# Counts of zero products on TensorE in a two-stage attention and wave-MLP kernel

## The chip, the cores and the metric

The kernel runs on one core of one Trainium2 chip. The metric is the device time of one execution in microseconds (us). The engines are named as in the profile: PE is TensorE's matrix products and PEld its weight loads, DVE is VectorE, ACT is ScalarE, POOL is GpSimd, SP is the engine that issues most transfers. L344 is line 344 of the kernel.

## The reference

Two blocks follow each other. The first is an attention with polynomial features, over 4 batches, 4 heads, 1088 positions and a head size of 32; the second mixes 1088 positions with two matrices, over the 128 channels that the heads make together.

```python
def phi(x):
    a = np.einsum('rd,bhsd->bhsr', S1, x)      # r = 8
    b = np.einsum('rd,bhsd->bhsr', S2, x)
    return np.einsum('bhsi,bhsj->bhsij', a, b).reshape(*x.shape[:-1], r * r)
q_p, k_p = (phi(q), phi(k))
kv = np.einsum('bhsf,bhsd->bhfd', k_p, v)
z = np.sum(k_p, axis=2)
num = np.einsum('bhsf,bhfd->bhsd', q_p, kv)
den = np.einsum('bhsf,bhf->bhs', q_p, z)[..., None] + 1e-06
x = num / den                                  # heads joined: (4, 1088, 128)
theta = x @ w_theta
y = einsum('ts,bsd->btd', w_tok_r, x * cos(theta)) + einsum('ts,bsd->btd', w_tok_i, x * sin(theta))
u = x + y
out = u + np.maximum(u @ w_ch, 0.0)
```

The arrays arrive in the types of the host; the matrices of the second block are 8-byte floats, which the kernel turns into 4-byte floats itself.

## The kernel before

Every step is recorded first as an operation with its engine, its buffers and a function that emits the instructions, and has a number. A list written out by hand, `SEQUENCE`, gives the order in which the recorded operations are emitted, and with it the order on each engine; each engine works through its own in order. A second list, `PLACES`, gives each buffer its slot, so a tile that is written again waits for the readers of the tile before in that slot. A third, `FILLS`, says in front of which operations PE gets extra products whose operands are zeroes and whose result nobody reads. A positive count writes the tile `nowhere`; a negative count writes the PSUM slot that the operation is about to use, which is asked for anew for each of these products:

```python
for o in self.order:
    n = self.fills.get(o.i, 0)
    for _ in range(n):
        fill()
    for b in o.bufs:
        if b.ap is None:
            b.ap = view(pools[b.cls](b.slot), b.shape, b.dt)
            if n < 0 and b.cls == "ps":
                for _ in range(-n):
                    fill(pools[b.cls](b.slot)[:, :GW_FILL])
                n = 0
    o.fn()
```

One such product (a fill, L378) is 128 x 128 weights by 384 columns in a 2-byte type. Eleven of them are an operation of their own at the very start, as soon as POOL has set `idle` to zero (L380). `FILLS` adds eight in front of operation 12.

The first operations, in PE's order of before: the 19 fills; operation 12, the transpose L431 of a small maximum `m` of the sketch matrices, for which DVE (L432, then L328) works out a power of two; the transposes L770 of the first batch of keys; four fills; the product L344 with `ones` that spreads that power of two; the transposes L993 of queries and L770 of keys; two fills; further transposes; a product for the size of the queries; and then the products of the first batch's rounded keys with themselves (`hf`, then `big`). Meanwhile ACT squares the keys with their sum (L673) and the queries (L969); DVE (L328) takes the step of the rounding from the keys' sum, rounds the keys and subtracts what was rounded (L324).

The middle, where the first stage ends: for each batch DVE multiplies the features of the queries out in three parts (tiles `g`, from `lv`, L324), PE transposes each part in two groups of three (L1127), ACT copies these (L1131), and PE multiplies them with the batch's keys and values. Operation 741 is the first such group of three of one batch; nine fills stand in front of it. The third part of a batch goes into the slot of its first part. Between these steps stand the unpacking of the matrices of the second block (ACT L609 and L611 from the loaded `zs` tiles, DVE L328 and L324, some additions as transfers by POOL, L338) and the products of the second block, `ps<-big,zs`, L344.

From about 107 us on, these products of the second block follow each other to the end, with a sum of matrix quarters in place of some of the products, and the output is stored batch by batch.

Of the kernel before, what the change touches and what calls it, by code (L numbers as in the profile page):

```python
# [116 lines left out]
)  # L117
FILLS = (
    (12, 8), (15, 4), (65, 1), (741, -9),
)  # L120


# [1434 lines left out]
```

## Time and profile before

| | us |
|---|---|
| median of 3 runs | 226.09 |
| lowest and highest | 226.06, 226.94 |
| profiled execution | 226.22 |
| its span, from the first to the last instruction | 224.4 |

| engine | busy us | share of the span | instructions |
|---|---|---|---|
| PE | 218.4 | 97% | 1502 |
| PEld | 181.6 | 81% | 1502 |
| DVE | 173.9 | 77% | 414 |
| ACT | 124.2 | 55% | 259 |
| POOL | 62.1 | 28% | 98 |

A share of busy time is a mean over stages with different limits, and a product of zeroes counts as busy. The 34 fills show as L378 with the tile `idle`; their profile groups have 9.9 us of busy time together. In a line of the timeline, the first figure is the start, the second the time to the end of the last of the merged instructions, and the bracket holds the idle time of that engine just before it, with the instruction that ended it.

### The profile page before, as it was taken

What the parts mean: (1) busy time and instruction counts of PE and PEld (TensorE: products, weight loads), DVE (VectorE), ACT (ScalarE), POOL (GpSimd) and SP (SyncE); (2) the same over time, 40 slices, a digit from 0 to 9 for tenths busy, and PEclk for the clock granted to TensorE, in tenths of its full rate; (3) what the DMA queues carried; (4) which work ended last, traced back from release to release, by engine and by line L of the source; (5) the groups of instructions that cost most, each with busy time, mean ns of one, the idle gap of its engine ahead of it and who ended that gap; (6) DMA issues with size and microseconds to landing.
All of it is one profiled execution on the core that took longest, in us unless ns stands there. A gap on an engine that the chain in (4) does not pass through costs nothing.

```text
span 224.4 us, 4128 instructions
## 1 busy us (share of the span) xinstructions
PE 218.4 (97%) x1502; PEld 181.6 (81%) x1502; DVE 173.9 (77%) x414; ACT 124.2 (55%) x259; POOL 62.1 (28%) x98
## 2 busy tenths in 40 slices
PE   7999999999999999999999999999999999999993
PEld 3798999998897496778888887888888888888882
DVE  3699999999999799999989987479770626723653
ACT  3898899599999599899989904760000000000000
POOL 1198920000007033048460277429500000000000
PEclk9999999999999999999999999999999999999999
DMA  3999999999459996998999799979992002341223
GB/s 116 413 418 407 410 339 329 409 417 423 130 191 256 267 286 186 195 251 159 192 239 324 135 182 196 193 128 183 190 181 48 0 0 37 66 71 28 50 41 61
DMA packets 31800, 45.71 MB, mean 204 GB/s; under 512 B 18852, under 2 KB 19108, under 8 KB 31652
## 3 DMA queue, kind: packets, MB, share of 16 engines
q1 hardware_dynamic: 24580, 30.30, 38.4%
q0 software_dynamic: 7200, 15.14, 37.2%
q8 instruction: 12, 0.20, 0.4%
q14 instruction: 8, 0.07, 0.1%
HBM read 28.07 MB, written 2.23 MB: 135 GB/s over the span
## 4 chain that ended last, share of the span: by engine, by line
PE 94%; DVE 3%; issue 1%; POOL 0%; DVEq 0%; POOLq 0%
PE ps L344 82%; PE ps L378 4%; PE ps L1127 2%; PE ps L1075 2%; PE ps L770 2%; PE ps L993 2%; DVE big L324 1%; DVE big L328 1%; DVE zs L324 0%; DVE sm L331 0%; DVE sm L328 0%; PE ps L938 0%; POOL idle L380 0%; DVE g L324 0%; PE ps L951 0%
## 5 line engine op out<-in xcount | busy, mean ns | idle before, releaser
L344 PE MATMUL ps<-big,zs 128*128 128x288 f32 (+2 forms) x498 | 115.6, 386 | 0.1
L344 PEld LDWEIGHTS ps<-big,zs 128*128 128x128 f32 x498 | 90.9, 190 | 20.3 <-DVE big L328 0.6
L338 POOL DMA_DIRECT2D big<-big x41 | 38.0, 1411 | 87.4 <-ACT sm L785 39.0
L609 ACT ACTIVATE big<-zs 128x544 f32<-128x544 f32 x32 | 22.1, 710 | 0.4 <-DVE big L324 0.3
L611 ACT ACTIVATE big<-zs 128x1088 int32<-128x1088 uint32 x16 | 19.2, 1217 | 0.0
L331 DVE SCALAR_TENSOR_TENSOR big<-ps,even,big 128x288 f32<-128x288 f32 (+2 forms) x23 | 10.6, 480 | 6.0 <-PE ps L344 5.8
L328 DVE TENSOR_SCALAR big<-big 128x544 int32<-128x544 int32 (+1 forms) x33 | 14.6, 461 | 0.5 <-ACT big L609 0.5
L344 PE MATMUL ps<-mf,big 128*128 128x96 f32 x72 | 14.4, 295 | 0.0
L331 DVE SCALAR_TENSOR_TENSOR big<-ps,big 128x288 f32<-128x288 f32 (+1 forms) x15 | 6.4, 439 | 10.1 <-PE ps L344 10.1
L338 POOL DMA_DIRECT2D big<-hf x9 | 12.9, 1928 | 0.1
L324 DVE TENSOR_TENSOR zs<-ps,g 128x768 f32<-128x768 f32 (+2 forms) x20 | 12.6, 629 | 0.1
L324 DVE TENSOR_TENSOR g<-lv 128x768 f32<-128x768 f32 x12 | 11.1, 954 | 1.8 <-PE ps L1127 1.7
L344 PEld LDWEIGHTS <-hf 128*128 128x128 f16 (+1 forms) x144 | 11.9, 106 | 0.5 <-issue 0.2
L324 DVE TENSOR_TENSOR big<-big,ps 128x288 f32<-128x288 f32 (+1 forms) x12 | 5.1, 427 | 8.6 <-PE ps L344 8.6
L378 PE MATMUL ps<-idle 128*128 128x384 bf16 x34 | 9.9, 415 | 1.8 <-POOL idle L380 1.3
L344 PE MATMUL ps<-w,big 128*128 128x128 f32 (+1 forms) x76 | 11.4, 285 | 0.0
L324 DVE CUSTOM_DVE_ANT_0 big<-big,big 128x1088 uint16<-128x1088 uint16 x16 | 11.3, 714 | 0.0
L344 PE MATMUL ps<-big,big 128*128 128x128 f32 x72 | 11.0, 283 | 0.0
L344 PEld LDWEIGHTS ps<-mf,big 128*128 128x128 f32 x72 | 10.9, 191 | 0.2 <-issue 0.2
L324 DVE TENSOR_TENSOR big<-big,hf 128x1152 f32<-128x1152 f32 x8 | 10.9, 1368 | 0.1
L344 PEld LDWEIGHTS ps<-w,big 128*128 128x128 f32 x76 | 9.8, 191 | 1.2 <-issue 0.6
L344 PE MATMUL ps<-mv,hf 128*128 128x96 f16 x108 | 10.6, 206 | 0.0
(196 smaller groups left out, 387.6 us busy)
## 6 DMA issues: line engine op xcount, KB each, us to landing
zs<-w_tok SPq DMA_DIRECT2D x17, 1088.0 KB, 12.2
big<-big POOLq DMA_DIRECT2D x40, 272.0 KB, 6.8
big<-k_l SPq DMA_DIRECT2D x7, 576.0 KB, 8.0
big<-q_l SPq DMA_DIRECT2D x4, 576.0 KB, 9.9
big<-v_l SPq DMA_DIRECT2D x4, 576.0 KB, 9.2
big<-hf POOLq DMA_DIRECT2D x3, 576.0 KB, 11.6
big<-hf POOLq DMA_DIRECT2D x6, 272.0 KB, 12.2
out<-g SPq DMA_DIRECT2D x32, 36.0 KB, 1.7
```

The lines of the kernel that those rows point to most:

```text
L324: eng.tensor_tensor(out=o, in0=a, in1=b, op=f)
L328: (eng or V).tensor_scalar(out=o, in0=a, scalar1=s1, scalar2=s2, op0=op0, **kw)
L331: (eng or V).scalar_tensor_tensor(out=o, in0=a, scalar=s, in1=b, op0=op0, op1=op1)
L338: op("G", n * 2.55e-3, lambda: G.dma_start(dst(), src(), accum_op=ALU.add), w, r, kind=2)
L344: T.matmul(o, lhs, rhs, start=start, stop=stop, skip_group_check=True)
L378: T.matmul(nowhere() if out is None else out, idle()[:, 0:P], idle(), start=True, stop=True, skip_group_check=True)
L609: op("A", 0.19 + HT * 0.0009, lambda j=j: A.activation(dst[j](), words()[1][:, j * HT:(j + 1) * HT].bitcast(F32), AF.Prelu, scale=scale, a ...
L611: op("A", 0.22 + S * 0.0009, lambda: A.activation(stp().rearrange("p r n -> p (r n)"), words()[0].bitcast(U32), AF.Copy, scale=2.0**-29), ...
L770: T.transpose(tr()[:, i * P:(i + 1) * P], kx()[:, g * GC + i].rearrange("p h d -> p (h d)"), ident())
L993: T.transpose(tr()[:, i * P:(i + 1) * P], x()[:, g * GC + i].rearrange("p h d -> p (h d)"), ident())
L1075: T.transpose(x()[:, i], xs()[:, off + i * P:off + (i + 1) * P], ident())
L1127: T.transpose(tr()[:, i * P:(i + 1) * P], qp()[:, i * H + 2 * n:i * H + 2 * n + 2].rearrange("p h i j -> p (h i j)"), ident())
```

## The change

Only the table of counts changes:

```diff
 FILLS = (
-    (12, 8), (15, 4), (65, 1), (741, -9),
+    (102, 3), (291, 3), (65, 1), (741, -4),
 )
```

The eleven fills at the very start stay. None follow them in front of L431 now; three stand between L431 and the first transposes L770 (operation 102), and three between the product with `ones` and the transposes L993 (operation 291), where four stood before that product. In front of operation 741 there are four instead of nine. The order of all other instructions, their buffers and the transfers are the same: PE has 11 products fewer, and as many weight loads.

## The prediction

> **What bounds the kernel now.** I read the page first: TensorE (PE) is busy 97% of the span. That is no answer yet, since products of zeroes count as busy. So next the busy time by stretches, for which engine has no idle time where:
>
> ```profile
> core 0: us, PE busy (x) PEld busy (x) DVE busy (x) ACT busy (x) POOL busy (x), PEclk, DMA share, GB/s
> 7.80:77.30 69.50, 68.69 (x663) 61.32 (x662) 67.24 (x164) 62.96 (x140) 21.95 (x47) 1.00 0.94 336
> 77.30:79.10 1.80, 1.63 (x11) 1.08 (x11) 0.12 (x2) 0.07 (x1) 0.00 (x0) 1.00 1.02 416
> 79.10:107.00 27.90, 27.78 (x217) 21.90 (x216) 27.46 (x54) 26.61 (x58) 11.17 (x14) 1.00 0.87 211
> 107.00:220.00 113.00, 113.00 (x587) 93.62 (x585) 75.55 (x165) 31.34 (x57) 27.71 (x32) 1.00 0.65 123
> ```
>
> Up to 107 us VectorE (DVE) works nearly without a pause, 67.24 of 69.50 us and 27.46 of 27.90; in the 1.80 us between, it does 0.12. After 107 us PE alone is full. So the time is a DVE stage, then a PE stage: what brings DVE forward in the first brings PE's start of the second forward. The list of waits on DVE confirms that the early stage has few holes. Its largest entries (15.9 and 15.0 us behind PE L344) cannot lie before 107 us, since DVE idles only 2.26 and 0.44 us there; these two can, and are the only waits that fills end:
>
> ```profile
> DVE sm L432 <- PE ps L431: 2.6, 1, 2.6
> DVE g L324 <- PE ps L1127: 1.7, 1, 1.7
> ```
>
> The timeline of the start (start, duration, engine, line, operation, idle time before it):
>
> ```profile
> 1.34 5.64 PE L378 MATMUL ps<-idle 128*128 128x384 bf16 x19 [1.34 <-POOL idle L380]
> ...
> 5.80 0.15 PEld L378 LDWEIGHTS <-idle 128*128 128x128 bf16 x1 [0.17 <-issue]
> 6.12 0.48 PEld L378 LDWEIGHTS <-idle 128*128 128x128 bf16 x3 [0.17 <-issue]
> 6.43 1.17 ACT L673 ACTIVATE big<-big 128x1152 f32<-128x1152 f32 x1 [1.69 <-DMA big<-k_l]
> ...
> 6.82 0.27 PE L431 MATMUL ps<-ident,m 128*2 128x128 f32 x1
> ...
> 7.13 0.28 DVE L432 TENSOR_REDUCE sm<-ps 2x1 f32<-2x128 f32 x1 [2.60 <-PE ps L431]
> ...
> 7.50 0.19 ACT L673 ACTIVATION_READ_ACCUMULATOR big<-big 128x1 f32 x1
> ...
> 8.14 0.32 DVE L328 TENSOR_SCALAR sm<-sm 128x1 int32<-128x1 int32 x2
> ```
>
> Nineteen fills hold PE until 6.82 us; only then comes the small transpose L431, whose operand DVE finished at 4.53 us (4.37 + 0.16, L450). Note the spacing of the weight loads: 0.32 us up to 6.12, then three in 0.48. PE runs at half pace until about 6.2 us, though the clock column prints 1.00.
>
> The timeline of the gap:
>
> ```profile
> 74.70 3.35 PE L378 MATMUL ps<-idle 128*128 128x384 bf16 x9
> ...
> 75.52 1.83 DVE L324 TENSOR_TENSOR g<-lv 128x768 f32<-128x768 f32 x2
> ...
> 78.12 1.53 PE L1127 MATMUL ps<-ident,g 128*128 128x128 f32 x12
> 79.03 1.25 ACT L1131 COPY g<-ps 128x384 f32<-128x384 f32 x3 [2.74 <-PE ps L1127]
> 79.03 0.96 DVE L324 TENSOR_TENSOR g<-lv 128x768 f32<-128x768 f32 x1 [1.68 <-PE ps L1127]
> ```
>
> DVE has its first product of lv ready at 75.52 + 0.96 = 76.48, but the transposes that read it start at 78.12, behind nine fills. DVE's third product goes into the first one's tile, so it waits for the six transposes that read that tile. ScalarE (ACT) waits beside it.
>
> **The change, part by part.** All sums are against the profiled execution: 226.22 us, a span of 224.4 and 1.82 around it. It lies 0.13 above the median of 226.09.
>
> *The gap, 9 fills to 4.* In the chain that ended last the fills stand at 75.09, 75.46, 75.84 and so on, 0.378 apart, because each waits for the one before on the same PSUM tile. Five fewer would free PE 1.9 us earlier: the fourth of them ends at 76.18. But then DVE's product at 76.48 is last. Where PE waits for such a product elsewhere (92.61 + 0.96 = 93.57, transposes at 93.71) 0.14 passes; after a fill, 0.04. So the transposes start at 76.52 to 76.62, the six take 0.89 as before, and DVE's third product starts 0.03 later, at 77.44 to 77.54 instead of 79.03. That is 1.49 to 1.59; I take 1.5. DVE's own second product ends at 77.35 (75.52 + 1.83), so 0.1 to 0.2 of the wait of 1.68 remains. ACT's copy at 79.03 moves by as much.
>
> *Does the 1.5 us last?* Next late is DVE itself, without holes to 107 us, then PE without holes. What could hold them is data that does not move along. The loads of w_tok (L604) issued at 72.81 and 75.84 take 7.4 us at most, so the later lands by 83.2. ACT first reads this pair at 87.14, or 85.3 when moved by 1.8: 2 us of cover; if it were gone, each us over would return as DVE idle time. The additions by DMA are issued by GpSimd when DVE or PE is ready, so they move too. I take all of it.
>
> *The start, 19 and 4 to 11, 3 and 3.* Eleven fills at 0.32 end at 1.34 + 3.52 = 4.86 us. L431 follows at once, 1.96 earlier; three more fills (0.96) end near 6.1, before the keys land (ACT's wait ends at 6.43). DVE's row of small operations, 7.13 to 8.22, goes to about 5.2 to 6.3. The operation at 8.14 needs only ACT's sum, ready at 7.50 + 0.19 = 7.69, so it starts at 7.72: 0.42 us. The two groups of three after it stand in place of four; they end before the square of the queries does (8.89 + 0.19 = 9.08), for which the next small product waits, so I cost them at nothing. If that cover were gone, two fills at half pace would cost 0.64.
>
> Not all of the 0.42 lasts. ACT waits for loads at 6.43 and at 7.82, and from there to 19.13 it idles for some 0.1 us, so it hardly moves. ACT L832 (18.62 + 0.42 = 19.04) gates PE's product at 19.36, which gates DVE at 20.02. PE can come 0.2 to 0.3 earlier there, and DVE has 0.13 of its own to lose. I take 0.3. The bounds are 0 (ACT holds all) and 0.9: how long the 19 fills take depends on when the pace doubles, and the runs shown differ by 0.88 (226.06 to 226.94).
>
> The sum: 1.5 + 0.3 = 1.8, so 226.22 − 1.8 = 224.4.
>
> **The clock, which speaks against the change.** The clock column is 1.00 throughout; half pace shows only in the spacing of 0.32 us before 6.2. In the gap of before PE gets one fill per 0.378 us, and the pace still held: the six transposes behind the fills take 0.89 us. With four fills, PE's stretch from 74.87 to 77.4 holds four fills and six transposes, with idle times of at most 0.4 us between them. By rows, then, no fall, and no term in the sum. The Trainium skill ("TensorE: Matmul & The Clock Gate", Part 1) says that the array starts at half clock, is let up by sustained activity, and falls back after an idle window of some 3.4 us; its Part 4 adds that transposes do not count as busy in the same way. By that rule the transposes that take the place of the five fills might count as idle, and the gap could become the place of a fall, which is the third rival below. No run here shows such a fall; the trace agrees with the slow start alone.
>
> **The rivals.**
> 1. *Transfers do not come forward.* GpSimd's additions wait for one another: the waits have POOL behind DMA for 7.9 us in three waits, and DVE behind DMA once, 0.5 us. If those after 107 us are paced by their queue, up to 1.8 us returns there as that wait, less what PE's queued work hides. Against it: the DMA share is 0.65 after 107 us and 0.87 before. Half lost: 225.3.
> 2. *The pace doubles late at the start.* Fewer fills before 6.2 us could delay the doubling. PE's work from 8.27 to 9.7 would then take 1.4 us more, and the first large product (10.92) would slip by up to that, while the early 0.3 is lost: 226.22 − 1.5 + 0.9 = 225.6, taking part as covered by PE's slack. Against it: fills, keys' transposes and fills follow each other in the changed order with 0.4 us of idle time.
> 3. *Slower: the clock falls in the gap.* Place: from the first transposes at 76.5. At the start half pace lasted from 1.34 to 6.2, 4.9 us; the same length here, in work that is 27.78 of 27.90 us PE, loses 2.4 us: 226.22 − 1.8 + 2.4 = 226.8. It decides against the change once half pace lasts over 3.6 us, and shows as slower once it lasts over 5.6. For a fall that lasts 6 us, between one length and two, it is 227.4, which I take. For it: five fills that kept PE busy go. Against: PE's idle time stays under 0.4 us at a time.
> 4. *The start brings more*, 0.9 instead of 0.3: 223.8.
>
> That the counts do not reach the program is no rival: the built order of PE has 11 fills, L431, 3, L770, L344, 3, and four in the gap.
>
> **How the numbers follow.** The forecast has 0.66, rival 1 0.10, rival 2 0.07, rival 3 0.11, rival 4 0.06. The likeliest is 224.4. Half a per cent of the median, about what a measurement of this kernel can tell from no change, is 1.13 us: faster is below 224.96, slower above 227.22. Faster: 0.64 of the forecast, 0.06 of rival 4, 0.04 of the halves of rivals 1 and 2: 0.74. Slower: most of rival 3, 0.09. The rest, 0.17, is the same. The range goes from 223.7, just past rival 4, to 225.9, past rivals 1 and 2; it leaves out rival 3 and the odd tails, some 0.17.
>
> **What would show it.** Right: L431 near 4.9 us; the wait of DVE L432 at about 0.7 instead of 2.6; DVE L328 at 7.7 instead of 8.14; four fills from about 74.4; L1127 right behind DVE's first product; the wait of DVE g L324 for L1127 at 0.1 to 0.2 instead of 1.7; PE's L344 of 84.98 near 83.2; the stretch to the end as long as before. Wrong: weight loads of fills 0.32 apart past 7 us or L344 products at twice their time after 76 us (rivals 2, 3); a DVE or ACT wait for DMA after 80 us (rival 1); no earlier DVE at 20 us (the early term is 0).

## The result: 224.73 us, and a wider spread than before

The changed kernel has a median of 224.73 us over 22 executions (224.09 to 228.07), the kernel before 226.26 over 22 (225.74 to 227.01): a ratio of 0.994, 95% interval 0.9921 to 0.9959. So it is faster, by 0.6%, and near the 224.4 of the forecast: 1.53 us were gained where 1.8 were forecast. But where these executions of before lie within 1.3 us of each other, those of the changed kernel do not: 14 lie from 224.09 to 225.26 (called short below), six from 225.61 to 226.89 (called long), two at 228.0. The ratio leaves out the two at 228.0, which had a granted clock of 0.99 and left no trace, and nothing below explains them. The profiled execution took 226.89 us (span 225.1), 0.67 more than the one before. It holds both the gain and what ate it.

The start, in the timeline of the changed kernel:

```profile
1.34 3.70 PE L378 MATMUL ps<-idle 128*128 128x384 bf16 x11 [1.34 <-POOL idle L380]
...
4.83 0.42 PE L431 MATMUL ps<-ident,m 128*2 128x128 f32 x1
...
5.29 0.28 DVE L432 TENSOR_REDUCE sm<-ps 2x1 f32<-2x128 f32 x1 [0.66 <-PE ps L431]
...
7.51 0.34 DVE L328 TENSOR_SCALAR sm<-sm 128x1 int32<-128x1 int32 x2 [1.13 <-ACT big L673]
```

The small transpose comes 1.99 us earlier, and the step of the rounding (L328) starts at 7.51 instead of 8.14. What holds it now is ACT's sum, as forecast.

The gap:

```profile
76.96 1.46 PE L378 MATMUL ps<-idle 128*128 128x384 bf16 x4
...
77.78 1.83 DVE L324 TENSOR_TENSOR g<-lv 128x768 f32<-128x768 f32 x2
...
78.88 1.72 PE L1127 MATMUL ps<-ident,g 128*128 128x128 f32 x12 [0.47 <-DVE g L324]
...
79.77 1.41 ACT L1131 COPY g<-ps 128x384 f32<-128x384 f32 x3 [1.22 <-PE ps L1127]
79.77 0.96 DVE L324 TENSOR_TENSOR g<-lv 128x768 f32<-128x768 f32 x1 [0.16 <-PE ps L1127]
```

DVE's first product ends at 77.78 + 0.96 = 78.74, and the transposes follow at 78.88. DVE's third product waits 0.16 us, where it waited 1.68. Ahead of the gap the whole kernel runs late, 77.78 against 75.52 for DVE's first product, +2.26; behind it +0.74, 79.77 against 79.03. The gap gave 1.52. In stages, cut at the corresponding places of the changed kernel:

```profile
7.80:79.60 71.80, 68.09 (x662) 61.19 (x661) 67.10 (x162) 62.71 (x140) 19.59 (x45) 1.00 0.92 325
79.60:79.80 0.20, 0.17 (x3) 0.08 (x2) 0.04 (x2) 0.04 (x1) 0.00 (x0) 1.00 0.94 392
79.80:107.70 27.90, 27.90 (x218) 22.21 (x219) 27.46 (x54) 26.71 (x58) 11.14 (x14) 1.00 0.93 234
107.70:220.70 113.00, 113.00 (x587) 93.62 (x586) 75.48 (x165) 31.26 (x57) 27.70 (x32) 1.00 0.65 123
```

The columns are those of the stretches of before: length, busy time of PE, PEld, DVE, ACT and POOL, then the clock. The last two stretches are as long as before and as full, 27.46 of 27.90 us for DVE and 113.00 of 113.00 for PE. In the first, DVE does 67.10 us of work as before (67.24), in 71.80 us instead of 69.50. There the time went, and PE's timeline shows the place:

```profile
31.80 0.33 PE L344 MATMUL ps<-sm,ones 128*128 128x1 f32 x2
34.80 1.53 PE L344 MATMUL ps<-g,big 128*64 128x128 f32 x24 [2.67 <-ACT big L609]
```

Before, the same product started with no wait:

```profile
32.25 1.53 PE L344 MATMUL ps<-g,big 128*64 128x128 f32 x24
```

The page names ACT L609, one of which ran from 34.10 to 34.80 us. But the product does not need that one: before, it started at 34.34, two us after the product. One operand of the product is the first batch's values, which SP loads with an issue at 14.87 us. The trace's semaphore records have the last part of this load at 34.67, 0.13 us before the product starts; before, it was there at 30.14, 2.1 us ahead of the product. Experiments below name that load outright, again with 0.14 us between its last part and the product. The clock is not it: behind the stall the 24 products take 1.53 us, as in a short execution of the change (from 31.80 us there). GpSimd's order had moved as well. GpSimd before, then after:

```profile
20.50 2.01 POOL L324 TENSOR_TENSOR mv<-c,hm 128x32 f16<-128x32 f16 x4
22.48 1.03 POOL L324 TENSOR_TENSOR mf<-cf,hm 128x32 f32<-128x32 f32 x2
23.45 1.06 POOL L338 DMA_DIRECT2D big<-hf  x1
```

```profile
19.88 0.83 POOL L324 TENSOR_TENSOR mv<-c,hm 128x32 f16<-128x32 f16 x4
20.67 0.44 POOL L324 TENSOR_TENSOR mf<-cf,hm 128x32 f32<-128x32 f32 x2
21.05 1.05 POOL L338 DMA_DIRECT2D big<-hf  x1
```

GpSimd was 0.6 us ahead, but its first addition by DMA (L338, 576 KB) went out 2.4 us ahead, since its small products took 1.2 instead of 3.0 us. The theory to test is this: the gap saves 1.5 us always; the start saves a few tenths, but in some executions lets this addition out early, and it takes DMA time from the load of the values that was queued first. Rival A: that load is late by chance, whatever the addition does. Rival B: the clock falls in some executions.

### The profile page after: what moved, and what is told of

Same layout as the page of the kernel before. It is cut to its first block, busy times and chain, and to the rows that moved or that the text cites. A ratio compares the mean times of both kernels' runs of the same rounds, so it can differ in the third digit from the quotient of the medians.

```text
span 225.1 us, 4106 instructions
## 1 busy us (share of the span) xinstructions
PE 216.3 (96%) x1491; PEld 180.4 (80%) x1491; DVE 174.3 (77%) x414; ACT 124.1 (55%) x259; POOL 60.0 (27%) x98
## 4 chain that ended last, share of the span: by engine, by line
PE 71%; DVE 17%; DMA 5%; ACT 2%; SPq 2%; issue 1%; DVEq 0%
PE ps L344 66%; DVE g L324 5%; DMA big<-q_l 4%; PE ps L1127 3%; DVE sm L331 2%; DVE big L328 2%; DVE sm L324 1%; DVE big L324 1%; PE ps L1075 1%; DVE lv L324 1%; SPq L651 1%; DVE hf L328 1%; PE ps L770 1%; DVE zs L324 1%; DMA out<-g 1%
## 5 line engine op out<-in xcount | busy, mean ns | idle before, releaser
L338 POOL DMA_DIRECT2D big<-big x41 | 38.0, 1410 | 87.0 <-ACT sm L785 40.8
L609 ACT ACTIVATE big<-zs 128x544 f32<-128x544 f32 x32 | 22.3, 715 | 0.9 <-DMA zs<-w_tok 0.6
L328 DVE TENSOR_SCALAR big<-big 128x544 int32<-128x544 int32 (+1 forms) x33 | 14.4, 455 | 0.5 <-ACT big L609 0.5
L338 POOL DMA_DIRECT2D big<-hf x9 | 12.9, 1918 | 3.2 <-DMA big<-k_l 3.1
L324 DVE TENSOR_TENSOR zs<-ps,g 128x768 f32<-128x768 f32 (+2 forms) x20 | 12.5, 626 | 0.1
L344 PE MATMUL ps<-g,big 128*64 128x128 f32 x144 | 9.2, 277 | 2.7 <-ACT big L609 2.7
L324 DVE TENSOR_TENSOR big<-big,ps 128x288 f32<-128x288 f32 (+1 forms) x12 | 5.1, 426 | 8.6 <-PE ps L344 8.6
L324 DVE TENSOR_TENSOR g<-lv 128x768 f32<-128x768 f32 x12 | 11.1, 951 | 0.3 <-PE ps L1127 0.2
L324 DVE CUSTOM_DVE_ANT_0 big<-big,big 128x1088 uint16<-128x1088 uint16 x16 | 11.2, 712 | 0.0
L324 DVE TENSOR_TENSOR big<-big,hf 128x1152 f32<-128x1152 f32 x8 | 11.0, 1370 | 0.1
```

What stands on the lines that cost most here:

```text
L324: eng.tensor_tensor(out=o, in0=a, in1=b, op=f)
L328: (eng or V).tensor_scalar(out=o, in0=a, scalar1=s1, scalar2=s2, op0=op0, **kw)
L338: op("G", n * 2.55e-3, lambda: G.dma_start(dst(), src(), accum_op=ALU.add), w, r, kind=2)
L344: T.matmul(o, lhs, rhs, start=start, stop=stop, skip_group_check=True)
L609: op("A", 0.19 + HT * 0.0009, lambda j=j: A.activation(dst[j](), words()[1][:, j * HT:(j + 1) * HT].bitcast(F32), AF.Prelu, scale=scale, a ...
```

## The experiments

The kernels ran in three groups of four, each group on one chip with its own runs of before: medians of before are 226.28 (the two halves, addition later, addition earlier), 226.49 (the four from "change again" on) and 226.42 (the last four). In these groups the executions of before spread over 1.4 to 1.7 us. All times are medians, with the range, in us; ratios are against before.

| kernel | time | ratio, 95% interval |
|---|---|---|
| gap alone | 224.90 (224.27 to 225.52) | 0.9933 (0.9909 to 0.9957) |
| start alone | 225.91 (225.46 to 229.52) | 0.9983 (0.9966 to 1.0) |
| change, addition later | 224.22 (224.01 to 225.12) | 0.9909 (0.9884 to 0.9933) |
| before, addition earlier | 227.71 (227.03 to 230.91) | 1.0075 (1.0043 to 1.0108) |
| change again | 224.49 (224.10 to 224.77) | 0.9903 (0.9880 to 0.9925) |
| later, no fills in the gap | 224.50 (224.19 to 225.65) | 0.9915 (0.9889 to 0.9940) |
| later, no fills at the start | 225.56 (225.03 to 225.78) | 0.9952 (0.9932 to 0.9973) |
| change, values before queries | 224.68 (224.25 to 224.97) | 0.9911 (0.9890 to 0.9932) |
| change, addition forced early | 225.75 (225.41 to 227.79) | 0.9977 (0.9955 to 1.0) |
| forced early, values first | 225.38 (225.12 to 225.70) | 0.9945 (0.9926 to 0.9965) |
| change, third time | 224.38 (224.17 to 226.27) | 0.9913 (0.9881 to 0.9944) |
| change, addition later, again | 224.53 (224.01 to 224.68) | 0.9901 (0.9878 to 0.9925) |

**The two halves, each alone.**

```diff
 gap alone
-    (12, 8), (15, 4), (65, 1), (741, -9),
+    (12, 8), (15, 4), (65, 1), (741, -4),
 start alone
-    (12, 8), (15, 4), (65, 1), (741, -9),
+    (102, 3), (291, 3), (65, 1), (741, -9),
```

> The counts of the start stay as before (8 in front of operation 12, 4 in front of 15); only the nine in the gap become four. Theory (the gap gives 1.5 us in every execution; the lower values of the change come from it; the long executions of the change come from the start, whose earlier additions by DMA hold back the load of the first batch's values): about 224.7 us, 1.5 less than the kernel before, and its executions lie as close together as those of before (within 1.3 us); PE near 32 to 35 us has no stall before ps<-g,big. Rival A (the load of the values is late by chance, whatever the start): as widely spread as the change, 224.2 to 226.9. Rival B (long executions come from a clock that falls in the gap): widely spread too, with L344 or L1127 products at twice their time after 76 us in a long one.

> The counts of the start are those of the change (3 in front of operations 102 and 291); nine stay in the gap. Theory: median 0.1 to 0.3 us below the kernel before, and widely spread, with executions up to 2.5 us above the shortest; where a profile falls on a long one, PE waits 2 to 3 us before ps<-g,big near 32 us. Rival A: as widely spread as before plus what chance gives every kernel of this call alike. Rival B: as close together as before, since nine fills keep the gap busy.

The gap alone gains 1.38 us in the median, the start alone 0.37, with an interval that reaches no change; together 1.75, where the forecast had 1.5 and 0.3. The seven executions of the gap alone lie within 1.25 us of each other, as the theory had it. In the trace of the gap alone, DVE starts 0.39 us earlier than before in front of the gap and 1.91 earlier after it: 1.52 for the gap. Its 0.39 at the start is no work of the change, since its counts there were those of before: its 19 fills took 4.60 us instead of 5.64, since PE's pace doubled earlier. The start alone is less spread than expected: 11 of 12 executions lie within 225.46 to 226.79, one at 229.52. So the long executions came less often here than in the change, and this run alone does not show that they come from the start.

In the trace of the start alone the load of the values shows itself in the chain that ended last (start, duration):

```profile
14.96 17.02 DMA big<-v_l
```

It ends at 31.98, and PE's product behind it starts at 32.12, 0.38 us later against before than the instructions ahead of it. So the load can be the last to arrive even with the addition at 22.94 us. In the two short profiles of the change, below, its last part lands 0.9 us before PE's product: that is all the cover it has there.

**The addition moved, later and earlier.** GpSimd's order of operations: 23 are the products mv<-s, mv<-c and mf<-cf, 241 the first addition, 26 and 20 the small copies behind it, 139 the second addition.

```diff
 counts of the change, addition later
-   30, 23, 241, 26, 20, 139
+   30, 23, 26, 20, 241, 139
 counts of before, addition earlier
-   19, 30, 23, 241
+   19, 241, 30, 23
 counts of the change, addition forced early
-   30, 23, 241
+   30, 241, 23
```

> The change with one thing moved: on POOL the two small copies of the tiles mv and mf (operations 26 and 20) go ahead of the first addition by DMA (big<-hf, L338), so that it is issued some 2 us later, about 23 instead of 21.05 us, behind the loads of the queue of SP. Theory (the early addition takes the DMA engines from the load of the values): the stall of PE near 32 to 35 us goes away in all executions, 224.2 to 224.7 us, within 1.3 us of each other. Rival A (the loads are slow by chance): spread as in the change, 224.1 to 226.9. Rival C (the additions themselves are needed early): slower than 225, with DVE or PE behind DMA for the first addition.

> The kernel before, counts and all, with the first addition by DMA (big<-hf, L338) moved forward on POOL by two steps, so that it is issued near 20 to 21 us instead of 23.45. Theory (an early addition holds back the load of the values): executions up to 2.5 us longer than before, 226 to 228.7, with PE stalled before ps<-g,big near 32 to 35 us. Rival A: same as before, 226.2, no stall.

> The change with one thing moved: the first addition by DMA (big<-hf, L338) goes ahead of GpSimd's products mv<-s, mv<-c and mf<-cf, so that it is issued near 19.5 us in every execution. Theory (an early addition holds back the load of the first batch's values): all executions long, 225.4 to 227.5 and some near 228, with PE waiting 1 to 3 us for the load of v before ps<-g,big. Rival A (the loads are slow by chance): 224.5, as the change.

Moved later, to 23.86 and 23.99 us, the 12 executions of its two runs lie between 224.01 and 225.12; none is long. Moved earlier in the kernel before (19.14 us), with no other edit, all are longer than any run of before on the same chip but one: eight of 12 from 227.03 to 228.16, within the expected range, and four at 230.2 to 230.9, above it. Those four had a mean granted clock of 0.98 against 1.00, for which no run gives a cause. Forced early in the change (19.80 us), the shortest of 12 is 225.41, 1.3 above the shortest of the change. PE's timeline of the change with the addition forced early, and the chain that ended last:

```profile
33.30 1.53 PE L344 MATMUL ps<-g,big 128*64 128x128 f32 x24 [1.68 <-DMA big<-v_l]
```

```profile
14.87 18.30 DMA big<-v_l
```

Here the wait carries the name of the load. It was issued at 14.87, as in the first profile of the change, and landed at 33.17. PE's starts are 0.70 us ahead of before near 31 us and 1.05 behind from 35 us on: 1.75 lost, of which 0.29 is caught up by 60 us, and the gap then gives 1.5 back.

The same holds over all traces in which SP's order is unchanged. The load of the last batch's queries, which SP issues just before that of the values, took 14.7 to 15.7 us to land in the nine traces with the addition at 22.76 us or later, and 17.2 to 18.0 in the three with it at 21.05 us or earlier (the long execution of the change among them). For the load of the values, by the last of its semaphore records, it is 13.3 to 17.0 against 18.0 to 19.8 us. Among the nine it falls as the addition goes out later, from 16.1 us with it at 22.76 to 13.3 with it at 24.65, give or take 1 us. Rival A says that the addition does not matter; it is out.

**Why single executions go over the edge.**

The changed kernel was run twice more, unaltered.

> The changed kernel once more, unaltered, for its spread on the chip of the other runs of this call and for a second profile. Theory (a short execution has its first addition by DMA at about 22.9 us, since GpSimd's four products mv<-c are caught behind DVE's long L324; a long one has it at about 21.05, since DVE was held by PE and GpSimd slipped through): a profile of 224.1 to 224.8 shows L338 at 22.8 or later, mv<-c x4 at 2.0 us and no stall at ps<-g,big; one of 225.6 to 226.9 shows L338 near 21, mv<-c x4 at 0.83 and a stall of 1 to 2.7 us. Rival A (the loads are slow by chance): the time of L338 has nothing to do with the length.

> The changed kernel, unaltered, on the chip of this call. Theory: 224.1 to 224.8 where GpSimd's products are caught behind DVE's long L324, and single executions of 225.5 to 227 where they are not. In the profile L338 is at 22.8 or later if the time is below 225, near 21 if it is above 225.5. Rival A: no such relation.

Both profiles fell on short executions (224.77 and 224.48), with the addition at 23.02 and 22.76 us and no wait of PE before ps<-g,big. One detail was expected wrong: in both, it is not mv<-c that is caught, but mf<-cf. DVE and GpSimd of the third run of the change:

```profile
19.88 0.83 POOL L324 TENSOR_TENSOR mv<-c,hm 128x32 f16<-128x32 f16 x4
...
20.51 1.41 DVE L324 TENSOR_TENSOR big<-big,hf 128x1152 f32<-128x1152 f32 x1
...
20.67 2.14 POOL L324 TENSOR_TENSOR mf<-cf,hm 128x32 f32<-128x32 f32 x2
...
22.76 1.06 POOL L338 DMA_DIRECT2D big<-hf  x1
```

Against the long execution, whose DVE had this line:

```profile
20.91 1.42 DVE L324 TENSOR_TENSOR big<-big,hf 128x1152 f32<-128x1152 f32 x1
```

In both, GpSimd starts mv<-c at 19.88 and mf<-cf at 20.67. In the short one DVE's long subtraction began 0.16 us before mf<-cf, whose two products then lasted 2.14 us, past the end of the subtraction (21.92) and through DVE's rounding step behind it (21.84 to 22.71), up to 22.81. In the long one DVE began at 20.91, behind a wait of 0.27 for PE that the short one does not have. Most of mf<-cf was done by then: it lasted 0.44, and the addition went out 1.7 us sooner. The Trainium skill ("GPSIMD Engine Reference", section 8, Key points) says that GpSimd shares its SBUF interfaces with VectorE and meets contention when a DVE instruction has two SBUF inputs; this subtraction has two, and the trace agrees with 2.14 against 0.44 us, as far as the subtraction goes; what held the products through the rounding step is not settled here.

In the two further runs of the change, one of 13 executions was long (226.27), without a trace. So the link between a long execution and an early addition rests on one long profile, two short ones and the runs that force it. That each long execution has this cause is not shown, nor how often it comes: 8 of the first 22 executions lie above 225.5, 1 of these 13.

**Where a stall goes when its load comes first.** The loads of the last batch's queries (operation 39) and of the first batch's values (33) change places on SP's queue, once with the counts and the order of the change, once with the addition forced early.

```diff
-   39, 33
+   33, 39
```

> The change with one thing moved: on the queue of SP the load of the first batch's values goes ahead of the load of the last batch's queries, which stood just in front of it; additions as in the change. Theory (the values land too late for ps<-g,big): they land about 3 us earlier, the stall near 32 us is gone even where L338 is issued near 21 us, and the executions lie at 224.0 to 224.9, provided that the queries, now 3 us later, are not missed. Rival A (the loads are slow by chance): spread as in the change.

> As the kernel with the addition forced early, and besides the load of the first batch's values goes ahead of the load of the last batch's queries on the queue of SP. Theory (the values are what the early addition holds back): their load lands some 2.4 us earlier, the wait before ps<-g,big is gone or under 0.5 us, and 1 to 2 us of the loss come back: 224.3 to 225.2. Rival D (the early addition costs through GpSimd's later products mv and mf, not through the load): as slow as without the exchange.

The first is inconclusive: its profile has the addition at 23.03, and there was nothing to remove; its time, 224.68, lies in the expected range. The second gives 225.38 where 224.3 to 225.2 was expected. The wait for the values is gone (ps<-g,big at 31.72, no idle time), but ACT now waits for the other load:

```profile
33.77 1.17 ACT L969 ACTIVATE big<-big 128x1152 f32<-128x1152 f32 x1 [2.51 <-DMA big<-q_l]
```

PE's starts go from 0.53 ahead at 35 us to 1.00 behind at 39 us. So the loss moves to the load that now comes second. That speaks for the theory, and against rival D, which had the cost in GpSimd's products.

The later addition has a price of its own. In its second profile PE waits for the addition itself, as rival C of its first expectation had it, though without the time above 225 that this rival gave:

> The variant with the addition issued later (GpSimd's copies of mv and mf ahead of it), on the same chip as the change, to compare the two. Theory: no execution above 225.3; median equal to the short executions of the change or up to 0.3 us below. Rival A: spread as the change.

```profile
34.72 0.71 PE L344 MATMUL ps<-big,big 128*128 128x128 f32 x4 [0.38 <-DMA big<-hf]
```

PE went there from 0.58 ahead of before to 0.13 ahead, and by 39 us it was 0.11 behind. Its median, 224.53, is no better than the 224.38 of the change on the same chip. None of its 12 executions is long, but it takes no time from the short ones; and against 1 of 13 for the change in the later runs, 12 executions are too few to say that it ends the long ones.

**The fills that stay.** On the kernel with the later addition:

```diff
 no fills in the gap
-    (102, 3), (291, 3), (65, 1), (741, -4),
+    (102, 3), (291, 3), (65, 1),
 no fills at the start
-    (102, 3), (291, 3), (65, 1), (741, -4),
+    (65, 1), (741, -4),
```

> The variant with the first addition issued later (the change, with GpSimd's copies of mv and mf ahead of it), and none of the four fills left in the gap. Theory (DVE's product at 76.48 of before is last once four are there, so fewer bring nothing): 224.2, as with the four. Rival (without fills the granted clock falls in the gap): 0.5 to 2.4 us more, 224.7 to 226.6, with the six transposes L1127 taking over 0.89 us.

> The variant with the first addition issued later, and none of the six fills (3 in front of operation 102, 3 in front of 291) at the start; the four in the gap stay. Theory (the fills at the start only keep the clock rising; without them the weight loads of PE stay 0.3 us and more apart past 7 us): first big product later by 0.3 to 1.4 us than with them (10.0 there), 224.4 to 225.3 in all. Rival (the clock rises by the eleven alone): 224.2, as with them.

Without any fill in the gap the time is 224.50, where 224.2 was expected; the change on the same chip had 224.49. In its profile PE idles 1.76 us there, and the pace holds:

```profile
76.06 1.72 PE L1127 MATMUL ps<-ident,g 128*128 128x128 f32 x12 [1.76 <-DVE g L324]
```

Twelve transposes take 1.72 us, as in the change, and the gap gives 1.52 us here too: DVE goes from 0.57 to 2.09 ahead of before. The four fills are worth nothing that was measured, and rival B does not hold in the gap of this execution.

Without the six at the start it is 225.56, above the 224.4 to 225.3 expected and 1.07 longer than the change on the same chip. PE's timeline there:

```profile
6.36 0.91 PE L770 MATMUL ps<-ident,big 128*128 128x128 f32 x3 [1.10 <-DMA big<-k_l]
...
9.13 0.85 PE L378 MATMUL ps<-idle 128*128 128x384 bf16 x2
```

These three transposes take 0.55 us in the change, the two fills 0.49 at 8.38. Here the pace is still half past 9 us, and the first big product starts at 11.56 instead of 10.21 to 10.48 in the three profiles of the change. The Trainium skill ("TensorE: Matmul & The Clock Gate", Part 1) says that the array is let up to full clock by about 3.4 us of sustained activity in a window that runs on its own; the idle 1.10 us, just when the pace doubles in the other kernels (4.2 to 6.5 us), agrees with it. That the idle time is the reason is argued, not shown: in one profile of the change PE idles 1.05 us at the same place and keeps full pace, which it had reached at 4.2 us.

## Why the prediction was right, and where it was not

- **The bound.** Right: what DVE gained before 107 us stayed to the end, and the two later stretches kept their 27.90 and 113.00 us.
- **The gap, 1.5 us.** Right in size and in its working: 1.52 in the profile of the change and with the gap alone. The wait of DVE L324 is 0.16 (0.1 to 0.2 forecast). The transposes start 0.14 after DVE's product, the upper of the two values taken.
- **"Does the 1.5 us last?"** Yes: the shift of +0.74 behind the gap is +0.73 at the end.
- **The start, 0.3 us.** The first steps came as worked out: L431 at 4.83 (4.9), L328 at 7.51 (7.72; the keys landed 0.2 us earlier than in the profile of before). The size is not contradicted, but not shown either: it is 0.37 alone by the medians, with an interval that reaches no change, and 0.18 and 0.45 by DVE's starts at 40 us in the two short profiles of the change. The gap alone, with the start of before, was 0.39 ahead too, because the pace of its fills doubled earlier; so a single profile cannot tell a term of 0.3. The two groups of three cost nothing that was seen, but they are needed: without them 1.07 us is lost.
- **What failed** is the step that says what of the 0.42 lasts. It followed DVE, ACT and PE from 7.8 to 20 us and stopped there. GpSimd's queue and SP's loads were followed only behind the gap ("they move too. I take all of it"). The step left out is at 19.9 to 35 us: GpSimd moves with DVE, one of its products passes or does not pass DVE's subtraction, an addition goes out 1.7 to 2.4 us sooner, and a load with little cover lands late. Price: 2.74 us in the profiled execution (PE went from 0.19 ahead of before to 2.55 behind, and caught up 0.29 by 60 us), 1.75 where the addition is forced early. It belonged into the first rival, which looked for such a loss behind 107 us only.
- **Rival 2** (the pace doubles late) had a mechanism that exists: without the six fills at the start the pace was still half past 9 us. Its 0.9 was counted against before; there PE is 0.43 behind before from 30 to 75 us, about half of that. The fills of the change keep it away. **Rival 3** (the clock falls in the gap) was seen in no profile, not even without fills there. **Rival 4** (0.9 from the start) was not seen.
- **The range**, 223.7 to 225.9, holds the median. Six of the 22 executions lie above it, the profiled one by the step left out; the other five left no trace. That the median still came within 0.3 us of the forecast is in part luck: the step left out struck in the smaller part of the executions only.

## What to carry to other kernels

Fills in front of an instruction are worth removing as far as the next latest operand: here 1.9 us were freed and 1.5 kept, and removing the rest changed nothing that was measured. When an early stage is brought forward by a few tenths, follow every queue that it releases, GpSimd's and the loads' too: here 0.6 us of lead on GpSimd became a wait of 2.67 us on TensorE, at a load that has 0.9 us of cover in the short executions. And where the executions of a kernel spread, profile a short one beside a long one before choosing a cause.

## What the runs showed of the hardware

- A transfer issued by GpSimd delays loads that SP had issued 3 to 8 us before: with the addition at 21.05 us or earlier the load of the last batch's queries took 17.2 to 18.0 us from its issue, with it at 22.76 us or later 14.7 to 15.7. The Trainium skill ("DMA: Bandwidth & Descriptors", Queues, rings and completion order) says that each DMA engine takes turns between the queues it has work for; the longer times agree.
- Two GpSimd products that take 0.44 us lasted 2.14 when they met a DVE subtraction of 1.41 us and the step behind it.
- PE's pace doubled anywhere from 4.2 to 6.5 us with nothing changed in the counts of the start, so that 19 fills took 4.60, 5.64 and 5.87 us in three profiles.
- The page put a wait of 2.67 us down to an ACT instruction that happened to end as the wait did, at 34.80 us. The last part of the load that PE needed landed at 34.67, and in two other traces the same wait carries that load's name.
